# A list-scheduled linear-attention and MLP kernel: new per-unit delays, a new table of tile places and ten new scheduler constants

## The chip, the cores and the metric

One Trainium2 chip, of which the program uses 1 core. The metric is device time in microseconds (us) of that core. The profile shows one execution of the program; the times are of other executions of it.

## The reference

Linear attention with exponential features, then an MLP without bias. There are 8 batches, 8 heads, 576 positions, 64 channels per head and 128 random features; the MLP has 4608 tokens of 512 channels and 2048 hidden units.

```python
def phi(x):
    proj = np.einsum('bhsd,df->bhsf', x, w_phi)
    proj = proj - np.max(np.abs(proj), axis=-1, keepdims=True)
    return np.concatenate([np.exp(proj), np.exp(-proj)], axis=-1)
q_p, k_p = (phi(q), phi(k))
kv = np.einsum('bhsf,bhsd->bhfd', k_p, v)
z = np.sum(k_p, axis=2)
num = np.einsum('bhsf,bhfd->bhsd', q_p, kv)
den = np.einsum('bhsf,bhf->bhs', q_p, z)[..., None] + 1e-06
x = (num / den).transpose(0, 2, 1, 3).reshape(B * S, H * D)
h = x @ w_in
out = (0.5 * h * (1.0 + erf(h / sqrt(2)))) @ w_out
```

## The kernel before, in words

**Attention.** Heads go in pairs, so each batch b has four pairs, made of two groups g with two halves p each. For the keys of one (b, g, p), `k_quad` loads `kt` and `vt`, TensorE (PE) multiplies `kt` with the feature weights `wst` into the PSUM tile `pk`, VectorE (DVE) takes the largest absolute value `mx` and subtracts it (`ek`), ScalarE (ACT) makes both exponentials, and PE sums them with the values into the PSUM tile `kv`, which ACT copies to `kvn`. The last 64 positions of all heads of a batch go through `k_rest` first (`kr`, `pk_r`, `er`), and every `kv` begins with their part. For the queries, `q_front` loads `qt`, PE makes `pq`, ACT copies it to `pc`, GpSimd (POOL) finds the largest absolute value over the partitions (`mb`, a partition_all_reduce, line 539), DVE subtracts it from `pc` and ACT makes both exponentials `ef` (line 544). PE then makes the products `pn` with `kvn`, copied by ACT to `xo`; for the first three batches PE also makes the denominators `dn`, copied to `do`. For later batches GpSimd sums them (`db`, line 550). In a name such as pq_0_3_1 the numbers are batch, pair and half of the positions (keys: batch, group, half); `rest` is the last 64 positions. In batch 0 both halves have 288 positions, in the other batches the first half has 512.

**Weights.** They come as 64-bit numbers. `split_weight` takes one piece: a load `raw` (line 413), ACT's absolute value (line 416), four VectorE instructions (lines 417, 419, 421, 423) that make a 32-bit number `wt`, a rounded cast on ACT (line 395) and the remainder on VectorE (line 401). There are 16 pieces of `w_i` and 16 of `w_o`.

**MLP.** It works on 18 blocks of 256 tokens. In blocks 0 to 7 PE multiplies the tokens' high and low parts `xh`, `xl` with `w_i` into `ph`, ACT and VectorE make the gelu's high and low parts `gh`, `gl`, and PE multiplies these with `w_o` into `po`. Blocks 8 to 17 form the second product from seven smaller ones (`pa`, `pb`, with sums of weights `tw`). The first `ph` stands between the attention of batches 1 and 2, since it needs the tokens of batch 0 alone; from there on the attention's PE work lies between matmuls of the blocks.

**What sets the order.** No order is written out by hand. Each operation is recorded by `Plan.op` with its engine, a hand-set cost, the tiles that it reads and writes, and a rank, to which the delay of its unit of work is added (`k01` is the keys of batch 0, half 1; `q220` the queries of batch 2, pair 2, half 0; `w_o3` a piece of weights; `b5_1` a part of a block). `Plan.order` is a list scheduler over all engines: among the operations that can start, it takes the one of lowest rank, and `Plan.emit` writes the instructions of each engine in that order. SP's queue carries nearly all DMAs, in planned order too. `Plan.pool` says in which buffer a tile lies: in the one of its own tag, unless the table `HOME` names another.

```python
def new(shape, dt, name):
    home = HOME.get(name, tag)
...
o.rank += DELAY.get(self.unit, 0.0)
...
pq = ps["pp"]([P, 2, 512], F32, f"pq_{nm}")
...
acc = ps["kv"]([P, 4, D + 1], F32, f"kv_{nm}_{p}")
```

A tile has to wait until the one before it in its buffer has been read for the last time. During the attention the PSUM places are `ph` (two), `po`, `pp`, `kv` and `pn` (one each); a `pk` or `pq` lies in `pp`, a `kv` or `dn` in `kv`, a `pn` in `pn`, unless `HOME` says otherwise. In SBUF, the places of weights that haven't come yet (`w_i0_0` to `w_o15`) serve as buffers for tiles of the attention. So the table `HOME` decides which waits on a buffer there are, and the order of two tiles on PE decides which comes first in one place.

All matmuls are recorded at line 360, the tensor-tensor operations of VectorE at line 401, copies and casts at 395 and 397. The change touches only the tables and constants from line 934 on; the scheduler reads them in `Plan.op`, `Plan.pool` and `Plan.order`.

Of the kernel before, what the change touches and what calls it, by code (L numbers as in the profile page):

```python
# [315 lines left out]
def fused_kernel(ctx: ExitStack, tc: tile.TileContext, qT, kT, va, w_st, w_in, w_out, out):  # L316
# [693 lines left out]
}  # L1010
SEVEN = 8
SUMS = 2
SUMSAT = 175.933
SUMSEACH = 3.384
SUMSPAN = 581.86
T15 = 870.02
T18 = 997.68
BIAS = 551.516
STICK = 2
PATIENCE = 2.138  # L1020
URGE = -1000.0
EARLY = 41.32
WPACE = 4.989
# [5 lines left out]
LUMP = 82.289  # L1029
# [56 lines left out]
```

## Time and profile before

| what | value |
|---|---|
| times of three runs | 1045.68, 1046.75, 1046.44 us; median 1046.44 us |
| profiled execution | 1048.43 us; span 1046.6 us; 1.83 us around the span |
| mean granted TensorE clock in it | 0.993 of full |
| busy in the span | PE 1019.6, VectorE 661.1, ACT 614.5, GpSimd 276.9 us |
| moved from and to HBM | 75.87 MB read, 29.66 MB written |

The profiled execution took 1.99 us longer than the median. Busy times of different engines lie beside one another, so they don't add up to the span. "PE" is the time with a matmul in the array, "PEld" its loads of weights, which overlap matmuls. The granted clock is given as a share of 2.4 GHz: 1.00 is that, 0.50 is 1.2 GHz.

### The profile page before, as it was taken

How to read it: one execution, taken by the hardware profiler on the slowest of the kernel's cores; microseconds unless marked ns; L12 is line 12 of the kernel's file. 1: busy time of each engine (PE TensorE's matmuls, PEld its weight loads, DVE VectorE, ACT ScalarE, POOL GpSimd, SP SyncE). 2: the span in 40 equal slices, each digit the busy share in tenths (PEclk: the TensorE clock that was granted, in tenths of full speed). 3: DMA queues.
4: the chain of work that ended last, by engine and by line, in shares of the span. 5: the costliest groups of instructions: out<-in, count | busy, mean ns of one | idle time of the engine just before them, and what ended most of it. 6: DMA issues, size and time to landing. Idle time of an engine off the chain costs nothing.

```text
span 1046.6 us, 24197 instructions
## 1 busy us (share of the span) xinstructions
PE 1019.6 (97%) x10070; PEld 893.1 (85%) x10070; DVE 661.1 (63%) x1209; ACT 614.5 (59%) x1011; POOL 276.9 (26%) x72
## 2 busy tenths in 40 slices
PE   6889998999999999999999999999999999999998
PEld 5555776878878878897887889999999999999998
DVE  5899999987777854334643433555564556474754
ACT  5788888886768766757755642343243334243433
POOL 2343331373376352326566540000000000000000
PEclk9899999999999999999999999999999999999999
DMA  8775654524534433222321339201111111110000
GB/s 294 216 231 170 208 189 119 164 88 140 162 123 147 152 108 91 67 76 72 97 72 39 97 107 326 60 22 41 44 39 40 43 42 42 41 42 19 24 22 21
DMA packets 87327, 107.11 MB, mean 102 GB/s; under 512 B 29021, under 2 KB 57245, under 8 KB 87217
## 3 DMA queue, kind: packets, MB, share of 16 engines
q1 hardware_dynamic: 86928, 105.30, 32.7%
q8 instruction: 79, 1.29, 0.5%
q14 instruction: 32, 0.25, 0.1%
q10 hardware_dynamic: 288, 0.26, 0.1%
HBM read 75.87 MB, written 29.66 MB: 101 GB/s over the span
## 4 chain that ended last, share of the span: by engine, by line
PE 90%; DVE 5%; ACT 2%; issue 1%; DMA 1%; SPq 0%; DVEq 0%; ACTq 0%
PE ph L360 38%; PE po L360 17%; PE pa L360 10%; PE pb L360 7%; PE kv L360 6%; PE pn L360 4%; PE pk L360 3%; PE pq L360 3%; PE dn L360 1%; DVE wt_i L421 1%; PE pn_rest L360 1%; DMA vt<-in_va_dram 1%; DVE ek L401 0%; DVE wt_i L423 0%; DVE pc L401 0%
## 5 line engine op out<-in xcount | busy, mean ns | idle before, releaser
L360 PE MATMUL ph<-xh,w_i 128*128 128x256 f32 x2304 | 416.6, 278 | 0.0
L360 PEld LDWEIGHTS ph<-xh,w_i 128*128 128x128 f32 x2304 | 357.1, 188 | 9.0 <-issue 5.1
L360 PE MATMUL ph<-xl,w_i 128*128 128x256 f32 x1152 | 319.3, 277 | 0.0
L360 PEld LDWEIGHTS ph<-xl,w_i 128*128 128x128 f32 x1152 | 217.2, 189 | 0.3
L539 POOL PARTITION_ALL_REDUCE mb<-pc x36 | 120.6, 3356 | 202.3 <-ACT pc L395 153.3
L360 PE MATMUL po<-w_o,gh 128*128 128x512 f32 (+1 forms) x519 | 162.4, 395 | 0.0
L550 POOL PARTITION_ALL_REDUCE db<-pc x20 | 124.2, 6212 | 93.7 <-DVE pc L600 89.9
L360 PEld LDWEIGHTS po<-w_o,gh 128*128 128x128 f32 x519 | 93.3, 188 | 30.0 <-issue 8.5
L401 DVE TENSOR_TENSOR sg<-ga 128x256 f32<-128x256 f32 (+1 forms) x240 | 84.3, 376 | 54.1 <-ACT ga L839 50.3
L360 PE MATMUL pa<-w_o,oh 128*128 128x256 f32 x640 | 112.6, 276 | 0.0
L401 DVE TENSOR_TENSOR gl<-ph,gh 128x512 fp32r<-128x512 f32 x64 | 43.5, 687 | 90.7 <-ACT ph L750 90.6
L360 PE MATMUL po<-w_o,gl 128*128 128x512 f32 (+1 forms) x275 | 100.8, 378 | 0.0
L360 PEld LDWEIGHTS pa<-w_o,oh 128*128 128x128 f32 x640 | 96.3, 188 | 0.1
L839 ACT ACTIVATE ga<-ph 128x512 f32<-128x512 f32 x80 | 47.8, 597 | 82.3 <-PE ph L360 52.1
L401 DVE TENSOR_TENSOR ul<-sg,uh 128x384 fp32r<-128x384 f32 x80 | 44.6, 558 | 71.5 <-ACT uh L395 70.3
L360 PE MATMUL pa<-w_o,ol 128*128 128x256 f32 x320 | 88.3, 276 | 0.0
L360 PE MATMUL pb<-tw,uh 128*128 128x256 f32 x464 | 82.9, 276 | 0.1
L544 ACT ACTIVATE ef<-pc 128x1024 f32<-128x1024 f32 (+1 forms) x72 | 68.1, 973 | 14.2 <-DVE pc L401 10.3
L470 ACT ACTIVATE ek<-ek 128x1024 f32<-128x1024 f32 x64 | 67.6, 1059 | 11.1 <-DVE ek L401 10.2
L395 ACT CAST uh<-sg 128x384 fp32r<-128x384 f32 x80 | 41.0, 512 | 50.6 <-PE pb L360 25.3
L360 PEld LDWEIGHTS pb<-tw,uh 128*128 128x128 f32 x464 | 69.9, 188 | 0.3 <-DVE ob L401 0.3
L360 PE MATMUL pn<-ef,kvn 128*64 128x512 f32 (+1 forms) x288 | 64.9, 571 | 1.9 <-ACT do L395 0.8
(93 smaller groups left out, 1591.5 us busy)
## 6 DMA issues: line engine op xcount, KB each, us to landing
vt<-in_va_dram SPq DMA_DIRECT2D x32, 325.0 KB
t_d<-ts SPq DMA_DIRECT2D x40, 256.0 KB
out_dram<-ob SPq DMA_DIRECT2D x34, 256.0 KB
kt<-in_kT_dram SPq DMA_DIRECT2D x32, 256.0 KB
raw_i<-in_w_in_dram SPq DMA_DIRECT2D x16, 512.0 KB
raw_o<-in_w_out_dram SPq DMA_DIRECT2D x16, 512.0 KB
qt<-in_qT_dram SPq DMA_DIRECT2D x28, 256.0 KB
x_d<-xo SPq DMA_DIRECT2D x28, 256.0 KB
```

What stands on the lines that cost most here:

```text
L360: return tc.keep_in_program_order(nc.tensor.matmul(*a, **kw))
L395: op(eng, cost, lambda: nc.scalar.copy(out=dst(), in_=src()), r=r, w=w, **kw)
L401: op(eng, cost, lambda: e.tensor_tensor(out=dst(), in0=a(), in1=b(), op=o), r=r, w=w, **kw)
L421: op("dve", dve(512), lambda: v.scalar_tensor_tensor(out=t(), in0=low(), scalar=29, in1=t(), op0=ALU.logical_shift_right, op1=ALU.bitwise_ ...
L470: op("act", act(256 * n), lambda s=s: nc.scalar.activation(e[s](), e[1](), AF.Exp, scale=1.0 - 2.0 * s), r=[e[1]], w=[e[s]], table="exp", ...
L539: op("pool", plan.SPENT[most], lambda: nc.gpsimd.partition_all_reduce(mb(), pc(), P, bass_isa.ReduceOp.absmax), r=[pc], w=[mb], port=most, ...
L544: op("act", act(2 * n), lambda s=s: nc.scalar.activation(ef[s](), pc(), AF.Exp, scale=1.0 - 2.0 * s), r=[pc], w=[ef[s]], table="exp", **k())
L550: op("pool", plan.SPENT[total], lambda: nc.gpsimd.partition_all_reduce(db(), pc()[:, :2], P, bass_isa.ReduceOp.add), r=[pc], w=[db], port= ...
L839: op("act", act(2 * TB, True) + 0.037, lambda ph=ph, ga=ga: nc.scalar.activation(ga(), ph(), AF.Gelu), r=[ph_all], w=[ga], table="gelu", a ...
```

## The change

No operation is added, removed or reshaped. All 360 entries of `DELAY` have new numbers; of `HOME`'s 210 entries 33 stand as they were, and the new table has 224. Ten constants of the scheduler change. The diff is cut to the constants and to the lines of the tables that matter below; `q001` is the unit of the queries of batch 0, pair 0, second half.

```diff
 DELAY = {
...
-    "q030": -1607.8, "r00": -1909.3, "q001": -2026.1, "q011": -1929.5, "q021": -1199.6, "q031": -113.1, "r01": -1069.1, "w_i0_0": -1260,
+    "q030": -2405.8, "r00": -2479.3, "q001": -3437.1, "q011": -2634.2, "q021": -2588.7, "q031": -1127.7, "r01": -2527.4, "w_i0_0": -711.3,
...
 HOME = {
...
-    "kv_0_0_1": "ph", "kt_0_1_0": "gh", "vt_0_1_0": "ef", "kt_0_1_1": "w_o9", "vt_0_1_1": "pc", "mx_0_1_0": "w_o14", "ek_0_1_0_1": "w_o13",
...
-    "ef_1_0_0_0": "w_i1_2", "ef_1_0_0_1": "w_i0_2", "dn_1_0_0": "ph", "xo_1_0_0": "mb", "do_1_0_0": "mb", "qt_1_1_0": "w_i3_3", "pq_1_1_0": "po",
...
-    "kt_1_1_0": "xl", "vt_1_1_0": "db", "kt_1_1_1": "w_i3_2", "pk_1_1_0": "po", "mx_1_1_0": "w_o14", "ek_1_1_0_1": "w_i2_3", "ek_1_1_0_0": "w_i1_3",
...
-    "pc_2_2_0": "ek", "mb_2_2_0": "w_o12", "ef_2_2_0_0": "w_o14", "dn_2_2_0": "pn", "xo_2_2_0": "gh", "do_2_2_0": "pc", "pc_2_3_0": "mb",
...
+    "ek_0_0_1_1": "w_i1_3", "ek_0_0_1_0": "w_o8", "kv_0_0_1": "ph", "kt_0_1_0": "kt", "vt_0_1_0": "w_i2_3", "kt_0_1_1": "xl", "vt_0_1_1": "ef",
...
+    "do_0_3_0": "w_o15", "qt_0_0_1": "pc", "pq_0_0_1": "po", "pc_0_0_1": "ef", "mb_0_0_1": "w_o8", "ef_0_0_1_0": "w_i0_2", "ef_0_0_1_1": "w_i2_3",
...
+    "mb_0_3_1": "w_i1_2", "ef_0_3_1_0": "pc", "ef_0_3_1_1": "w_i0_3", "pn_0_3_1": "kv", "dn_0_3_1": "pn", "xo_0_3_1": "w_i2_2", "do_0_3_1": "w_i0_2",
...
+    "qt_1_0_0": "w_o11", "pq_1_0_0": "po", "pc_1_0_0": "w_o12", "mb_1_0_0": "w_o13", "ef_1_0_0_1": "xl", "pn_1_0_0": "kv", "xo_1_0_0": "w_o10",
...
-SUMSAT = 175.933
-SUMSEACH = 3.384
+SUMSAT = 174.271
+SUMSEACH = 2.354
...
-BIAS = 551.516
+BIAS = 702.831
...
-PATIENCE = 2.138
+PATIENCE = 2.126
...
-WPACE = 4.989
+WPACE = 5.047
...
-LUMP = 82.289
-LINGER = 6.494
+LUMP = 67.602
+LINGER = 6.464
...
-HOLD = 23.07
+HOLD = 21.532
...
-DMASLACK = 0.517
+DMASLACK = 0.686
```

Places of the tiles that the prediction names, where the table before or after says something else than the tag: pq_0_0_1 lay in `pp` and lies in `po`; dn_0_3_1 in `kv`, now `pn`; dn_2_2_0 in `pn`, now `kv`; dn_1_0_0 in `ph`, now `kv`; pn_1_0_0 in `pn`, now `kv`; vt_1_1_0 in `db`, now in the places of its own tag.

The order of the instructions moves on every engine up to about 190 us of the span before, and is the same from there on.

**ACT's queue at the first copy of key sums** (`kvn_0_0_0` is that copy; the last number of a name, here and below, only tells tiles apart). Before:

```order
L544 ACTIVATE ef_0_0_0_0_261<-pc_0_0_0_179 128x576
L544 ACTIVATE ef_0_0_0_1_263<-pc_0_0_0_179 128x576
L416 ACTIVATE wt_i0_0_266<-raw_i0_0_143 128x512
L395 COPY kvn_0_0_0_270<-kv_0_0_0_215 128x260
L416 ACTIVATE wt_i1_0_277<-raw_i1_0_147 128x512
L470 ACTIVATE ek_0_0_1_0_290<-ek_0_0_1_1_268 128x1024
L470 ACTIVATE ek_0_0_1_1_268<-ek_0_0_1_1_268 128x1024
```

and now:

```order
L544 ACTIVATE ef_0_0_0_0_257<-pc_0_0_0_175 128x576
L544 ACTIVATE ef_0_0_0_1_265<-pc_0_0_0_175 128x576
L416 ACTIVATE wt_i0_0_267<-raw_i0_0_141 128x512
L544 ACTIVATE ef_0_1_0_1_272<-pc_0_1_0_184 128x576
L416 ACTIVATE wt_i1_0_274<-raw_i1_0_145 128x512
L470 ACTIVATE ek_0_1_0_0_277<-ek_0_1_0_1_270 128x1024
L395 COPY kvn_0_0_0_282<-kv_0_0_0_216 128x260
L470 ACTIVATE ek_0_1_0_1_270<-ek_0_1_0_1_270 128x1024
L470 ACTIVATE ek_0_0_1_0_296<-ek_0_0_1_1_280 128x1024
```

The copy stood behind one piece of weights (L416); now one exponential for the queries (L544), a second piece of weights and one exponential for the keys (L470) stand ahead of it as well.

**SP's queue around the load of vt_1_1_0** (the values for the keys of batch 1, group 1, half 0). Before, where it was the 59th issue:

```order
L592 DMA d_d0_1_775<-do_0_0_1_768 4x144
L664 DMA dc_0_0_778<-d_d0_0_512 128x18
L712 DMA xr_0_521<-x_d0_3_0_666 128x256
L413 DMA raw_i2_1_828<-in_w_in_dram 128x512
L496 DMA vt_1_1_0_845<-in_va_dram 128x650
L477 DMA kr_2_849<-in_kT_dram 128x2x128
L563 DMA qt_1_1_0_867<-in_qT_dram 128x512
```

and now, where it is the 26th:

```order
L563 DMA qt_0_2_0_263<-in_qT_dram 128x288
L413 DMA raw_o0_291<-in_w_out_dram 128x512
L496 DMA vt_0_1_0_293<-in_va_dram 128x650
L494 DMA kt_1_0_0_309<-in_kT_dram 128x512
L496 DMA vt_1_0_0_311<-in_va_dram 128x650
L496 DMA vt_1_1_0_314<-in_va_dram 128x650
L477 DMA kr_1_316<-in_kT_dram 128x2x128
```

The load moved 33 places forward, out of a stretch of stores and weights into one of loads. Likewise `wst` was the 6th issue of the queue and is the 4th.

**PE's queue around the end of batch 2** (pk_3_0_0 and the like are the first keys of batch 3). Before:

```order
L360 MATMUL po_0_1403<-w_o11_2080,gl_0_5_2041 128x512
L360 MATMUL pk_3_0_0_2120<-wst_124,kt_3_0_0_1755 128x128 x8
L360 MATMUL pn_2_2_0_2134<-ef_2_2_0_0_2057,kvn_2_1_0_1870 64x512 x2
L360 MATMUL pn_2_2_0_2134<-ef_2_2_0_1_2082,kvn_2_1_0_1870 64x512 x2
L360 MATMUL dn_2_2_0_2155<-ef_2_2_0_0_2057,kvn_2_1_0_1870 32x256 x4
L360 MATMUL dn_2_2_0_2155<-ef_2_2_0_1_2082,kvn_2_1_0_1870 32x256 x4
L360 MATMUL pk_3_0_1_2175<-wst_124,kt_3_0_1_2140 128x128 x8
L360 MATMUL pn_2_3_0_2188<-ef_2_3_0_0_2173,kvn_2_1_1_2131 64x512 x2
L360 MATMUL pn_2_3_0_2188<-ef_2_3_0_1_2116,kvn_2_1_1_2131 64x512 x2
```

and now:

```order
L360 MATMUL pq_2_rest_2086<-qt_2_rest_1901,wst_120 128x256 x2
L360 MATMUL pn_2_2_0_2092<-ef_2_2_0_0_2036,kvn_2_1_0_1870 64x512 x2
L360 MATMUL pn_2_2_0_2092<-ef_2_2_0_1_2061,kvn_2_1_0_1870 64x512 x2
L360 MATMUL dn_2_2_0_2104<-ef_2_2_0_0_2036,kvn_2_1_0_1870 32x256 x4
L360 MATMUL dn_2_2_0_2104<-ef_2_2_0_1_2061,kvn_2_1_0_1870 32x256 x4
L360 MATMUL pk_3_0_0_2122<-wst_120,kt_3_0_0_1759 128x128 x8
L360 MATMUL po_0_1400<-w_o10_1948,gh_0_5_1987 128x512 x2
L360 MATMUL po_0_1400<-w_o10_1948,gl_0_5_2100 128x512
L360 MATMUL po_0_1400<-w_o10_1948,gh_0_5_1987 128x512 x2
```

The key projection pk_3_0_0 stood ahead of pn_2_2_0 and dn_2_2_0, with pk_3_0_1 directly behind them; now it stands behind them, and twelve `po` matmuls follow it before the next attention piece. Further on, pn_2_rest and dn_2_rest were followed by dn_2_3_0 and then kv_3_0_0; now dn_2_3_0 stands ahead of them and kv_3_0_0 directly behind.

## Rows read from the trace of the kernel before

**Rows 1.** The page's busy times, share of the span and instructions of each engine.

```profile
PE 1019.6 (97%) x10070; PEld 893.1 (85%) x10070; DVE 661.1 (63%) x1209; ACT 614.5 (59%) x1011; POOL 276.9 (26%) x72
```

**Rows 2.** Windows: stretch, length, busy of PE, PEld, DVE, ACT, POOL, clock, DMA, GB/s.

```profile
20.00:40.00 20.00, 15.84 (x354) 12.18 (x352) 19.68 (x28) 17.44 (x32) 4.67 (x2) 1.00 0.63 196
40.00:60.00 20.00, 18.34 (x296) 13.00 (x296) 15.85 (x25) 16.09 (x28) 7.18 (x3) 0.83 0.78 240
60.00:80.00 20.00, 16.93 (x272) 9.93 (x272) 18.98 (x24) 15.91 (x27) 9.73 (x3) 1.00 0.72 242
80.00:100.00 20.00, 17.76 (x201) 12.46 (x197) 18.64 (x27) 17.02 (x25) 9.62 (x3) 0.91 0.50 139
100.00:120.00 20.00, 20.00 (x231) 15.58 (x229) 18.99 (x33) 16.62 (x28) 4.31 (x1) 1.00 0.74 234
```

**Rows 3.** View of waits, engine PE, whole span: the costliest of 14 lines.

```profile
PE pk_r L360 <- DMA wst<-in_w_st_dram: 6.3, 1, 6.3
```

**Rows 4.** Timeline of PE: start, us, operation, count, idle before and releaser.

```profile
18.99 1.19 PE L360 MATMUL pn<-ef,kvn 128*64 128x288 f32 x8 [0.48 <-ACT kvn L395]
...
40.52 2.29 PE L360 MATMUL pq<-qt,wst 64*128 64x288 f32 x8 [2.95 <-DVE ek L401]
...
42.73 2.19 PE L360 MATMUL pn<-ef,kvn 128*64 128x288 f32 x8
...
47.47 0.69 PE L360 MATMUL kv<-vt,er 128*64 128x65 f32 x16
...
61.19 0.69 PE L360 MATMUL kv<-vt,er 128*64 128x65 f32 x16 [2.33 <-DMA vt<-in_va_dram]
...
70.05 0.70 PE L360 MATMUL dn<-ef,kvn 128*32 128x144 f32 x16 [1.32 <-ACT xo L395]
...
83.69 1.29 PE L360 MATMUL dn<-ef,kvn 128*32 128x256 f32 x16 [2.24 <-ACT do L395]
...
159.22 1.07 PE L360 MATMUL dn<-ef,kvn 128*32 128x256 f32 x16 [1.73 <-ACT xo L395]
...
160.95 1.16 PE L360 MATMUL pk<-wst,kt 64*128 64x128 f32 x16 [0.66 <-DVE ek L401]
...
166.97 0.69 PE L360 MATMUL kv<-vt,er 128*64 128x65 f32 x16 [0.61 <-ACT do_rest L395]
```

**Rows 5.** A window of 2 us (columns as in rows 2), of a half-clock stretch.

```profile
42.00:44.00 2.00, 2.00 (x10) 0.77 (x8) 1.06 (x2) 1.62 (x3) 1.39 (x1) 0.50 0.64 127
```

**Rows 6.** Timeline of ACT around the first copy of key sums.

```profile
17.34 0.69 ACT L416 ACTIVATE wt_i<-raw_i 128x512 f32<-128x512 f32 x1
...
18.56 0.38 ACT L395 COPY kvn<-kv 128x260 f32<-128x260 f32 x1 [0.53 <-PE kv L360]
...
39.27 1.26 ACT L544 ACTIVATE ef<-pc 128x576 f32<-128x576 f32 x2 [0.88 <-DVE pc L401]
...
40.43 1.04 ACT L470 ACTIVATE ek<-ek 128x1024 f32<-128x1024 f32 x1
```

**Rows 7.** Timeline of VectorE: an idle gap, and two long instructions beside plain ones.

```profile
46.98 0.43 DVE L417 TENSOR_SCALAR wt_o<-wt_o 128x512 f32<-128x512 f32 x1 [3.89 <-ACT wt_o L416]
...
66.36 2.67 DVE L421 SCALAR_TENSOR_TENSOR wt_o<-raw_o,wt_o 128x512 uint32<-128x512 uint32 x1
...
68.95 0.68 DVE L421 SCALAR_TENSOR_TENSOR wt_i<-raw_i,wt_i 128x512 uint32<-128x512 uint32 x1
...
70.16 3.20 DVE L401 TENSOR_TENSOR pc<-pc,mb 128x1024 f32<-128x1024 f32 x1
...
76.94 1.22 DVE L401 TENSOR_TENSOR pc<-pc,mb 128x1024 f32<-128x1024 f32 x1
```

**Rows 8.** Timeline of GpSimd: two reductions.

```profile
66.31 7.33 POOL L539 PARTITION_ALL_REDUCE mb<-pc  x2 [3.40 <-ACT pc L395]
```

**Rows 9.** Timeline of SP's queue: issues of two loads.

```profile
3.09 0.43 SPq L390 DMA_DIRECT2D wst<-in_w_st_dram  x1
...
55.61 0.85 SPq L496 DMA_DIRECT2D vt<-in_va_dram  x1
```

134 rows, old and new, of tables (DELAY, HOME) are left out of this document.

## The prediction

> **What bounds the kernel now.** I read the busy times first: TensorE (PE) has a matmul in the array for 1019.6 of 1046.6 us [rows 1]. So at most 27 us of the span are idle on PE, and the question is where they lie. The windows of 20 us answer it: between 100 and 120 us PE is busy for 20.00 of 20 us, but 15.84, 18.34, 16.93 and 17.76 in the four before it [rows 2]. What lies behind 190 us has the same order after the change, so I price nothing there. In the windows before 100 us VectorE is as full as PE or fuller: 19.68, 18.98 and 18.64 us, and only 15.85 between 40 and 60 [rows 2]. The reader should see from this that up to the first `ph` two engines bound the kernel in turn: a wait that goes on PE is worth nothing unless VectorE then also has its work earlier.
>
> The view of waits says that PE's costliest wait is its first, 6.3 us for `wst` [rows 3]. The timeline of PE gives the others in their places [rows 4]: 2.95 us before pq_0_0_1, at 40.52; 2.33 us for vt_1_1_0 before kv_1_1_0, at 61.19; 1.32 us before dn_0_3_1, at 70.05; 2.24 us before dn_1_1_0, at 83.69, just ahead of the first `ph`; in batch 2, 1.73 us before dn_2_2_0, 0.66 before pk_3_0_1 and 0.61 before kv_3_0_0. The clock comes third. From 42 to 44 us it is granted at 0.50, the lower level [rows 5], and the 20 us from 40 and from 80 have 0.83 and 0.91 of it, where the others shown have 1.00 [rows 2]; in both of these PE had one long wait, 2.95 and 2.24 us. Eight `pn` matmuls take 2.19 us there, against 1.19 at full clock [rows 4].
>
> **The change, part by part.** The prices are made against the profiled execution, 1048.43 us, 1.99 above the median of 1046.44.
>
> *Start.* `wst` was issued sixth, at 3.09 us [rows 9], and is now fourth; `kr`, which the same matmuls read, goes from third to fifth. An issue takes 0.43 us and a little more, so the later of the two is one place, about half a us, earlier. Bounds 0 and 0.9 us gained; I take 0.5 and count it in the next term.
>
> *First copy of key sums, kvn_0_0_0.* PE's pn_0_0_0 waits for it at 18.99 us [rows 4]. Before, ACT had waited 0.53 us for PE ahead of this copy, behind one piece of weights [rows 6]. Now three pieces stand in between: an `ef` of 0.63 us (half of 1.26), a piece of weights of 0.69 and an `ek` of 1.04 [rows 6]. 0.63 + 0.69 + 1.04 - 0.53 = 1.8 us later, and everything behind pn_0_0_0 on PE waits with it. Walking on through the four queues in the new order, with the durations of the rows, I get more such short waits, and kv_0_1_1, which closes the keys of batch 0, 2.9 us later. That is an estimate; the bounds are 1.3 (the 1.8 less the half us of the start) and 4 (twice the 1.8, and a little).
>
> *pq_0_0_1.* It lay in `pp` behind pk_1_0_0, which VectorE had to read twice; it now lies in `po`, which is long free. The 2.95 us go. If PE does not idle there, the low clock behind it goes too: the 20 us from 40 were granted 0.83, so 0.17 x 20 = 3.4 us of PE work [rows 2]. 2.95 + 3.4 - 2.9 = 3.4 us ahead at kv_1_0_0 (47.47 before [rows 4]), the largest lead that the change gives. VectorE allows it: it stood idle for 3.89 us up to 46.98 [rows 7], the one long gap it has there, and that gap hung on the late PE.
>
> *vt_1_1_0, dn_0_3_1.* The load moved 33 places ahead, past weights and stores; it had been issued at 55.61 us, 5.6 before its use [rows 4, 9], and is now there long before. The 2.33 us go. The load that moves back for it, vt_0_1_0 (14th to 23rd issue), is needed only by kv_0_1_0, and is in the 2.9 above. dn_0_3_1 lay in `kv` behind pn_0_3_1 and now has `pn`: 1.32 go. But VectorE is full again from 47 us, and its pieces set when PE has work. By the walk, kv_1_0_1 is 1.8 us ahead, kv_1_1_0 and kv_1_1_1 0.7 each: most of the 3.65 us comes back as waits for ACT and VectorE. pn_1_0_0 now stands in `kv` directly behind kv_1_1_1, and dn_1_0_0 behind pn_1_0_0, so each waits for ACT's copy of the one before it: new, estimated at 1 us each, under the 1.73 and 1.32 that such waits cost here [rows 4]. dn_1_1_0 still stands behind two copies. The first `ph` comes at 83.6 instead of 84.9 (where dn_1_1_0 started at 83.69 and took 1.29): a lead of 1.3. Bounds: -1.5 (half of the 2.9 late isn't made up) and +3.9 (VectorE's whole gap).
>
> *The low clock at 84 us.* The 20 us from 80 have 0.91, so 1.8 us are lost [rows 2]. Whether the clock falls depends on how long PE waits ahead of `ph`, and that wait is shorter but not gone. I take half, 0.9; bounds 0 and 1.8.
>
> *Batch 2.* dn_2_2_0 lies in `kv` now, away from pn_2_2_0: 1.73 go. pk_3_0_1 has twelve `po` matmuls between itself and pk_3_0_0: 0.66 go. Against that, kv_3_0_0 lies in `kv` directly behind dn_2_rest; before, dn_2_3_0 lay between them on PE, and still 0.61 was left [rows 4]. Without that cover, which took about as long as dn_2_2_0's 1.07 us, its wait grows to 0.61 + 1.07. Net 1.73 + 0.66 - 1.07 = 1.3 us. PE is full there, so these count one to one. Bounds 0.3 and 2.4 (no new wait).
>
> *Unseen short waits* between 90 and 190 us, where every engine's order moved: -0.5; bounds -2 and 0. The other new places in SBUF I price at nothing: what covers them is the work of VectorE, full nearly throughout; where a load came late behind such a place, the price would be of the kind of vt_1_1_0's 2.33.
>
> Sum: 1.3 + 0.9 + 1.3 - 0.5 = 3.0 us gained. Profiled 1045.4; median 1046.44 - 3.0 = **1043.4 us**.
>
> **A rule against it.** In the rows the clock fell in the two stretches with waits of 2.95 and 2.24 us, and stayed at 1.00 from 60 to 80 us, with waits of 2.33 and 1.32 us in it [rows 2, 4]. The change trades few long waits for more short ones, and by these rows that is good. The Trainium skill, page "TensorE: Matmul & The Clock Gate", section "A second HAM failure mode: psum-queue depth-cycling", says the contrary of such patterns: frequent micro-idles between groups of matmuls make the clock go up and down. By it, the two terms on the clock would be lost and the time would be that of the slower rival below. No row here shows a fall after short waits alone.
>
> **The rivals.** *Same time.* VectorE, at 18.6 to 19.7 of 20 us outside its one gap [rows 2], sets the pace to the first `ph` and beyond, its work is unchanged, and the lead of 3.4 is eaten: 0 at `ph`, 1.3 from batch 2, 0.5 to 2 back for the unseen waits: about 1046, and 1044.4 to 1048.4 with 2 us either way. For it speaks that every later piece of `ph` work needs VectorE; against it the gap of 3.89.
>
> *Slower.* The late kvn_0_0_0 costs its 2.9 us, the walk's recovery at pq_0_0_1 does not happen since PE, waiting for short pieces, keeps or regains the low clock once more (1.8 us, what it lost at 84): 2.9 + 1.8, less the 1.3 of batch 2, is 3.4 more, **1049.8**. It is decided at kv_1_0_0: if that starts later than 47.5 us, this holds. For it: the new order puts at least six tiles directly behind one another in a bank. Against: one such wait is an ACT copy, 0.38 us [rows 6], and what stands ahead of it.
>
> *A larger gain.* While GpSimd reduces, some VectorE instructions take far longer: an L421 2.67 us where the next one takes 0.68, an L401 3.20 where a later one of its shape takes 1.22, both beside the two reductions from 66.31 to 73.64 [rows 7, 8]. If the new order puts other instructions beside these reductions, 2.0 + 2.0 = 4.0 us of VectorE time come back before the first `ph`, VectorE no longer eats the lead there, and 3.0 + 4.0 gives **1039.4**. The Trainium skill, page "GPSIMD Engine Reference", section "Specifications", says that GpSimd shares its SBUF interfaces with VectorE, and that instructions in a two-port mode or with two SBUF inputs contend with it; the two named are of the second kind. Against it: no trace shows yet what stands beside a reduction after the change, and as many such instructions remain to be done in the same time.
>
> That the change does nothing is excluded: four queues have another order.
>
> **How the numbers follow.** My forecast 0.46 (its own range 1040.5 to 1045.5), same time 0.25, slower 0.19, larger gain 0.10. The range of 8 in 10 takes in the larger gain, with 2 us below it, and the price of the slower case: 1037.5 to 1050.0. A measurement here can tell 0.2%, 2.1 us. Faster by more: 0.40 of the forecast's 0.46 and 0.10 make 0.50. Within it: 0.06 and 0.22 of the same-time case make 0.28. Slower: 0.19 and 0.03 make 0.22.
>
> **What would show it.** Right: no wait before pq_0_0_1 and full clock from 40 to 47 us; kv_1_0_0 near 44; no wait for `vt`; first `ph` near 83.6; dn_2_2_0 without a wait, kv_3_0_0 with some 1.7. Wrong: low clock anywhere between 20 and 80 us, kv_1_0_0 behind 47.5, a first `ph` behind 84.9 (slower) or before 80 (larger gain), or a new wait behind 190 us, where I price nothing.

## The result, and the profile after

| kernel | executions | median | lowest to highest | ratio to before, 95% interval |
|---|---|---|---|---|
| before | 22 | 1046.60 us | 1042.79 to 1050.90 | |
| the change | 22 | 1055.32 us | 1046.46 to 1058.81 | 1.0070 [1.0051, 1.0090] |

The change makes the kernel 0.7% slower, well beyond the 0.2% that a measurement can tell. The forecast was 1043.4, its range ended at 1050.0. The profiled execution after took 1058.81 us (span 1057.0, mean clock 0.990).

More telling than the median is the spread. Over three jobs (the 22 above, and the runs r1_again and r2_again below) the changed kernel was executed 42 times: **12 took 1046.46 to 1050.98 us (the lower group), 30 took 1053.77 to 1058.98 (the upper group), and none lay between.** The medians of the two groups are 1048.73 and 1056.16. The 131 executions of the kernel before in the jobs of this study fill 1042.35 to 1052.56 us with no gap over 1.4 us. So the question has two parts: what splits the executions, and why even the lower group gains nothing.

PE's view of waits of the profiled execution (it belongs to the upper group), the costliest of 16 lines:

```profile
PE pn L360 <- ACT kvn L395: 7.7, 2, 4.8
PE pk_r L360 <- DMA kr<-in_kT_dram: 5.7, 1, 5.7
PE pq L360 <- DVE ek L401: 3.1, 1, 3.1
PE pq_rest L360 <- issue: 2.4, 1, 2.4
...
PE kv L360 <- ACT do_rest L395: 0.5, 1, 0.5
```

The first wait, 6.3 us before [rows 3], is now 5.7 and ends with `kr`. The waits for `vt` and of `dn` [rows 4] are gone, as forecast, and the 2.95 us before pq_0_0_1 are 0.60, now for its load. New are 7.7 us for `kvn` and 3.1 for an `ek`. Their places in PE's timeline:

```profile
19.52 1.79 PE L360 MATMUL pn<-ef,kvn 128*64 128x288 f32 x8 [2.94 <-ACT kvn L395]
...
57.49 1.33 PE L360 MATMUL pq<-qt,wst 64*128 64x288 f32 x4 [3.08 <-DVE ek L401]
...
79.35 3.68 PE L360 MATMUL pn<-ef,kvn 128*64 128x512 f32 x8 [4.77 <-ACT kvn L395]
```

They are pn_0_0_0, pq_0_3_1 and pn_1_0_0. Behind each of them PE is at the lower clock, behind the first from 20 to 23 us. Three windows of 2 us (columns as in rows 2):

```profile
42.00:44.00 2.00, 2.00 (x36) 1.47 (x30) 0.64 (x2) 2.00 (x6) 2.00 (x1) 1.00 0.96 343
...
60.00:62.00 2.00, 2.00 (x18) 0.82 (x18) 0.99 (x2) 1.77 (x4) 1.65 (x1) 0.50 0.87 226
...
80.00:82.00 2.00, 2.00 (x8) 0.48 (x4) 1.94 (x4) 1.43 (x3) 0.00 (x0) 0.50 0.84 288
```

The window from 42 us had 0.50 before [rows 5] and has 1.00 now: that part of the forecast came true. But low clock returned at 20, at 60 and at 80 us, and the forecast had named low clock anywhere between 20 and 80 us as a sign of being wrong.

The chain of waits from 46 to 92 us shows what made the two waits (some of its 51 pieces):

```profile
49.91 6.18 DMA x_d<-xo
...
56.21 1.24 DVE ek L401
...
57.53 1.06 ACT ek L470
...
62.52 3.34 PE kv L360 x80
...
70.34 1.55 DVE wt_i L419
...
73.68 3.14 DVE pc L401
...
76.89 0.92 issue
77.81 0.26 ACT ef L544
...
79.02 0.29 ACT kvn L395
...
79.35 3.68 PE pn L360 x8
```

Two things stand out. A store of 144 KB took 6.18 us to land, and a VectorE subtraction, an `ek`, waited 1.95 us for it, since it writes where the store still read. And an L419 and an L401 on VectorE took 1.55 and 3.14 us of the chain, where their plain durations are 0.42 and 1.22 us.

**The two groups side by side.** VectorE and GpSimd (its two L539 rows) in the profiled execution of the upper group:

```profile
67.86 1.23 DVE L465 TENSOR_REDUCE mx<-pk 128x8 f32<-128x1024 f32 x1 [0.54 <-PE pk L360]
69.11 1.22 DVE L401 TENSOR_TENSOR ek<-pk,mx 128x1024 f32<-128x1024 f32 x1
70.26 1.63 DVE L419 TENSOR_SCALAR wt_i<-wt_i 128x512 uint32<-128x512 uint32 x1
...
73.61 3.21 DVE L401 TENSOR_TENSOR pc<-pc,mb 128x1024 f32<-128x1024 f32 x1
76.73 0.68 DVE L401 TENSOR_TENSOR er<-pk_r,mx_r 128x512 f32<-128x512 f32 x1
...
68.07 3.54 POOL L539 PARTITION_ALL_REDUCE mb<-pc  x1 [5.04 <-ACT pc L395]
73.55 3.54 POOL L539 PARTITION_ALL_REDUCE mb<-pc  x1 [1.94 <-ACT pc L395]
```

and in the profiled execution of r1_again, the same kernel, of the lower group (span 1048.7 us; the last line is PE's pn_1_0_0):

```profile
66.46 1.22 DVE L465 TENSOR_REDUCE mx<-pk 128x8 f32<-128x1024 f32 x1
67.71 1.23 DVE L401 TENSOR_TENSOR ek<-pk,mx 128x1024 f32<-128x1024 f32 x1
68.85 0.48 DVE L419 TENSOR_SCALAR wt_i<-wt_i 128x512 uint32<-128x512 uint32 x1
69.26 0.68 DVE L423 SCALAR_TENSOR_TENSOR wt_i<-raw_i,wt_i 128x512 uint32<-128x512 uint32 x1
69.86 0.68 DVE L421 SCALAR_TENSOR_TENSOR wt_i<-raw_i,wt_i 128x512 uint32<-128x512 uint32 x1
...
71.06 1.21 DVE L401 TENSOR_TENSOR pc<-pc,mb 128x1024 f32<-128x1024 f32 x1
72.19 0.68 DVE L401 TENSOR_TENSOR er<-pk_r,mx_r 128x512 f32<-128x512 f32 x1
72.79 2.08 DVE L423 SCALAR_TENSOR_TENSOR wt_i<-raw_i,wt_i 128x512 uint32<-128x512 uint32 x1
...
66.87 3.72 POOL L539 PARTITION_ALL_REDUCE mb<-pc  x1 [3.92 <-ACT pc L395]
72.15 3.54 POOL L539 PARTITION_ALL_REDUCE mb<-pc  x1 [1.55 <-ACT pc L395]
...
74.97 1.94 PE L360 MATMUL pn<-ef,kvn 128*64 128x512 f32 x8 [1.80 <-ACT kvn L395]
```

This is where the two differ; that it makes the groups is tested by y1 below. In the execution of the lower group VectorE comes late to mx_1_1_1 (no wait), its L419 starts 1.98 us after the start of GpSimd's first reduction and takes 0.48; the subtraction of pc_1_0_0 starts 1.09 us ahead of the second reduction and takes 1.21. In that of the upper group VectorE is early, waits 0.54 us for PE, L419 starts 2.19 us after that start and takes 1.63. So the subtraction starts 0.06 us behind the second reduction and takes 3.21 us, 2.0 more than it needs alone; such an instruction is called held here. ACT's `ef`, its copy kvn_1_1_1 and PE's pn_1_0_0 hang on it; PE waits 4.77 us instead of 1.80 in r1_again and then runs at half clock: eight `pn` take 3.68 us instead of 1.94. The instruction held in the lower group's execution is an L423, a piece of weights behind the subtraction, on which nothing near depends.

What is held agrees with the Trainium skill, page "GPSIMD Engine Reference", section "Specifications" (GpSimd contends with VectorE instructions in a two-port mode or with two SBUF inputs): `pc` and L423 have two SBUF inputs, and `mx` and `ek`, which read PSUM, took their usual 1.2 us beside the first reduction. L419 has one input; no row shows in which mode it runs.

The traces show more: it matters which part of a reduction an instruction meets. Instructions with two SBUF inputs that started 0.06 to 1.07 us into a reduction of 3.54 us took so much longer that, with their plain time at the end, they were let go 2.05 or 2.06 us after its start (twelve profiles; for the `pc` above, 0.06 + 3.21 - 1.21). Those that started at 2.38 us or later, in a reduction of 3.54 or 3.72 us, took their plain time, as L423 and L421 at 69.26 and 69.86 us in the profile of r1_again. L419, started at 2.19 us, was let go at 3.40 (2.19 + 1.63 - 0.42).

### The profile page after: what moved, and what is told of

The parts are those of the page before. It is cut to its first block, busy times and chain, and to the rows that moved or that the text cites. A ratio compares the mean times of both kernels' runs of the same rounds, so it can differ in the third digit from the quotient of the medians.

```text
span 1057.0 us, 24220 instructions
## 1 busy us (share of the span) xinstructions
PE 1025.8 (97%) x10074; PEld 895.1 (85%) x10074; DVE 664.6 (63%) x1209; ACT 617.1 (58%) x1013; POOL 275.7 (26%) x72
## 4 chain that ended last, share of the span: by engine, by line
PE 89%; DVE 3%; DMA 3%; ACT 3%; issue 2%; SPq 1%; DVEq 0%; ACTq 0%
PE ph L360 37%; PE po L360 16%; PE pa L360 10%; PE pb L360 7%; PE kv L360 6%; PE pn L360 5%; PE pq L360 3%; PE pk L360 3%; DMA t_d<-ts 1%; PE dn L360 1%; ACT ek L470 1%; DMA x_d<-xo 1%; PE pk_r L360 0%; DVE ob L401 0%; DVE ek L401 0%
## 5 line engine op out<-in xcount | busy, mean ns | idle before, releaser
L539 POOL PARTITION_ALL_REDUCE mb<-pc x36 | 122.4, 3402 | 204.1 <-ACT pc L395 143.0
L401 DVE TENSOR_TENSOR sg<-ga 128x256 f32<-128x256 f32 (+1 forms) x240 | 84.6, 376 | 62.0 <-ACT ga L839 58.8
L401 DVE TENSOR_TENSOR gl<-ph,gh 128x512 fp32r<-128x512 f32 x64 | 43.5, 686 | 89.9 <-ACT ph L750 89.8
L401 DVE TENSOR_TENSOR ul<-sg,uh 128x384 fp32r<-128x384 f32 x80 | 44.6, 558 | 67.0 <-ACT uh L395 65.8
L470 ACT ACTIVATE ek<-ek 128x1024 f32<-128x1024 f32 x64 | 67.7, 1059 | 17.7 <-DVE ek L401 17.0
L360 PE MATMUL pn<-ef,kvn 128*64 128x512 f32 (+1 forms) x288 | 67.4, 589 | 9.2 <-ACT kvn L395 7.7
L544 ACT ACTIVATE ef<-pc 128x1024 f32<-128x1024 f32 (+1 forms) x72 | 67.9, 972 | 12.8 <-DVE pc L401 11.1
```

What stands on the lines that cost most here:

```text
L360: return tc.keep_in_program_order(nc.tensor.matmul(*a, **kw))
L401: op(eng, cost, lambda: e.tensor_tensor(out=dst(), in0=a(), in1=b(), op=o), r=r, w=w, **kw)
L470: op("act", act(256 * n), lambda s=s: nc.scalar.activation(e[s](), e[1](), AF.Exp, scale=1.0 - 2.0 * s), r=[e[1]], w=[e[s]], table="exp", ...
L539: op("pool", plan.SPENT[most], lambda: nc.gpsimd.partition_all_reduce(mb(), pc(), P, bass_isa.ReduceOp.absmax), r=[pc], w=[mb], port=most, ...
L544: op("act", act(2 * n), lambda s=s: nc.scalar.activation(ef[s](), pc(), AF.Exp, scale=1.0 - 2.0 * s), r=[pc], w=[ef[s]], table="exp", **k())
```

## The experiments

In all of them the order is the planned order of the named kernel, written out as a list, and only the shown line differs. Each job has its own executions of the kernel before, and the ratios are to those.

**r1_again, the change unchanged.**

> The changed kernel, unchanged, executed again for a second profile. Theory of the late store (T1): VectorE's subtraction for the keys ek_1_1_0_1 waits about 2 us for the store of xo_0_0_1 (it landed at 56.1 us in the first profile), PE waits about 3 us before pq_0_3_1, and the clock is low from about 57 to 64 us; median again about 1055 us. If this execution is one of the quick ones (1046 to 1050 us), the store lands before 54 us and the low clock at 57 to 64 us is missing. Theory of the clock alone (T4): the waits stand at the same places and are equally long in a quick and a slow execution, and only the stretches of low clock differ.

Measured: median 1056.13 us of 10 (1049.32 to 1058.98), before 1047.20 of 30: 1.0071 [1.0047, 1.0095]. Three executions in the lower group, seven in the upper; the profile, shown above, is of the lower. It has the wait of pq_0_3_1 (1.9 us, with low clock behind it from 58 to 61 us), the place of pn_1_0_0 and the wait of pq_rest (2.3 us) in common with the other one, but not the held subtraction. So the theory of the late store missed: it wanted the low clock at 57 us to be missing in a quick execution.

**x1_ek_place: `ek` away from the store.** In the change ek_1_1_0_1 lies behind xo_0_0_1, whose store it must wait for. Its own place is that of before; new is that xo_0_0_1 lies there too (before, in `pc`).

```diff
-    "ek_1_1_0_1": "w_i2_3"
+    "ek_1_1_0_1": "w_o7"
```

> One entry of the table of places: ek_1_1_0_1 no longer lies in w_i2_3 behind xo_0_0_1, but in w_o7, which nothing has used yet; the order of all engines is that of the changed kernel, written out. T1 (late store): no wait of PE before pq_0_3_1, no low clock from 57 to 64 us, kvn_1_1_0 at about 61 us in place of 65.9, first ph at about 86 in place of 89.9, time about 5 us less than the changed kernel: 1050 us. T2 (the PSUM place of pn_1_0_0): the 4.8 us before pn_1_0_0 stay, time within 2 us of the changed kernel. T3 (the PSUM place of pq_1_rest): the 2.4 us before pq_1_rest stay and set the time, within 2 us.

Measured: 1048.96 us (1046.98 to 1057.67), 1.0036 [1.0010, 1.0062]; three of 10 are still in the upper group, and one lies between the groups (1052.12). In its profile the wait before pq_0_3_1 is 0.7 us and PE has no low clock from 40 to 80 us. So the upper group is rarer without the store's wait, but not gone: the store is not what makes it.

**x2_pqrest_place: the `issue` wait of 2.4 us.**

```diff
-    pq_1_rest in the place of its tag, "pp"
+    "pq_1_rest": "po"
```

> One entry: pq_1_rest lies in po in place of pp, as in the kernel before; order as in the changed kernel, written out. T3: the 2.4 us before pq_1_rest and the low clock at 102 to 105 us (1.7 us) go, time 4 us less than the changed kernel: 1051 us. T1 and T2: 0 to 2 us less, since what is late ahead of it stays late, and the next piece of PE then waits for VectorE.

Measured: 1056.13 us (1046.24 to 1058.82), 1.0072 [1.0044, 1.0100]: nothing. In its profile the 2.4 us became a wait of 2.2 for `gl` at the same place. A miss.

**x3_pn_place: pn_1_0_0 away from kv_1_1_1.**

```diff
-    "pn_1_0_0": "kv"
+    pn_1_0_0 in the place of its tag, "pn"
```

> One entry: pn_1_0_0 lies in its own place pn in place of kv behind kv_1_1_1; order as in the changed kernel, written out. T2: the 4.8 us before pn_1_0_0 shrink to 1 or less, the low clock at 78 to 84 us goes (3.3 us), time 5 to 7 us less: 1049 us. T1: pn_1_0_0 then waits for its exponentials, which come at 77.9 us instead of the copy at 79.3, so 1.4 us less wait, 0 to 2 us of time.

Measured: 1051.08 us (1047.48 to 1054.95, 9 executions), 1.0037 [1.0012, 1.0062]; 4 of 9 above 1052. The place costs a little, since kvn_1_1_1 stands behind `ef` on ACT, but the long wait is for `ef` itself.

**x5_ek_pn_place: both.**

> Both ek_1_1_0_1 in w_o7 and pn_1_0_0 in pn, order of the changed kernel written out. If the store and the PSUM place are two links of one chain, each alone took away 7 and 5 us of the median and both together take away little more than the first: 1047 to 1049, and none over 1054. If they are two causes of their own, the sum: 1044 or less.

Measured: 1047.88 us (1046.87 to 1053.89), 1.0016 [0.9998, 1.0033]. The median is in the expected 1047 to 1049. One execution of 10 was in the upper group, and it was the profiled one: the subtraction started 0.06 us behind the second reduction there too, and took 3.21 us. PE's pn_1_0_0 now waited 3.4 us for `ef`.

**y1_pc_first: the subtraction two places earlier, nothing else.** VectorE's order:

```diff
+L401 TENSOR_TENSOR pc_1_0_0<-pc_1_0_0,mb_1_0_0
 L421 SCALAR_TENSOR_TENSOR wt_i1_1<-raw_i1_1,wt_i1_1
 L465 TENSOR_REDUCE mx_2_r<-pk_2_r
-L401 TENSOR_TENSOR pc_1_0_0<-pc_1_0_0,mb_1_0_0
```

> One instruction of VectorE moved in the changed kernel's order (all else written out as it was): the subtraction of pc_1_0_0 stands two places further forward, ahead of one weight instruction (L421) and of the maximum for pk_2_r. Theory of the meeting (R): in the slow executions this subtraction starts just after GpSimd's second reduction (73.61 behind 73.55) and takes 3.2 us in place of 1.2, and the copy of kvn_1_1_1 behind it makes PE wait 4.8 us; moved forward it no longer meets it, so the slow executions get 3 to 5 us shorter: median 1051 to 1053. Theory of the clock alone (T4): the low clock from 57 to 64 us sets the slow executions, and the subtraction takes 3.2 us because all is late; median stays at 1055 to 1056.

Measured: **1048.73 us** (1045.88 to 1050.58), before 1046.55: 1.0015 [1.0002, 1.0028]. None of 10 in the upper group; 0.7% of loss became 0.15%. Its profile (VectorE, then GpSimd):

```profile
66.32 1.23 DVE L465 TENSOR_REDUCE mx<-pk 128x8 f32<-128x1024 f32 x1 [0.52 <-PE pk L360]
...
68.72 1.63 DVE L419 TENSOR_SCALAR wt_i<-wt_i 128x512 uint32<-128x512 uint32 x1
70.27 0.67 DVE L423 SCALAR_TENSOR_TENSOR wt_i<-raw_i,wt_i 128x512 uint32<-128x512 uint32 x1
70.87 1.21 DVE L401 TENSOR_TENSOR pc<-pc,mb 128x1024 f32<-128x1024 f32 x1
...
66.53 3.54 POOL L539 PARTITION_ALL_REDUCE mb<-pc  x1 [4.26 <-ACT pc L395]
72.02 4.06 POOL L539 PARTITION_ALL_REDUCE mb<-pc  x1 [1.95 <-ACT pc L395]
```

VectorE waited for PE and its L419 was held, as in the upper group, but the subtraction was all but over when the second reduction began (it ended at 72.08 us, the reduction started at 72.02).

**y2_reduce_waits: the second reduction made to wait for the subtraction**, by the place of its result.

```diff
-    "mb_1_1_0": "w_o9"
+    "mb_1_1_0": "w_o13"
```

> One entry of the table of places in the changed kernel, order written out as it was: the result mb_1_1_0 of GpSimd's second reduction lies where mb_1_0_0 lay, so that this reduction cannot start before VectorE has made the subtraction of pc_1_0_0 that reads mb_1_0_0. No instruction of any queue moves. Theory of the meeting (R): pc_1_0_0 takes 1.2 us in every execution, none is slower than 1052, median 1048 to 1049 as with the moved instruction. Rival: moving the subtraction helped because it stood earlier by two instructions (1.4 us) in VectorE's queue, not because of the meeting; then here GpSimd's reduction is 1.2 us later and nothing is won: median 1055 or more.

Measured: 1051.76 us (1046.13 to 1055.24), 1.0049 [1.0030, 1.0069], between the two theories; five of 10 were above 1052, where the theory of the hold had expected none. In the profile the subtraction took 1.21 us, but pn_1_0_0 still waited 2.77 us, and its eight matmuls took 3.48, at half clock. L419 was still held and made the subtraction late; in y1 the two places made up for that. So to take the second hold away alone gives half of it.

**h1 and h2: front and rear apart.** h1 has the changed order up to what is planned for 260 us, and behind it the order of before; h2 the reverse.

> Order of the changed kernel for what its plan starts in the first 260 us, and from there on the order of the kernel before; table of places of the changed kernel. From the traces, all executions of the changed kernel lose another 2.4 to 2.9 us between 290 us and the end against the kernel before, quick and slow alike. If the order of the rear does that, this kernel is 2.6 us quicker than the changed one: median 1053, quick ones 1044 to 1047. If it is a consequence of the front (of when data come), it stays at 1055 to 1056.

> The reverse: order and places of the kernel before for the first 260 us, then the order of the changed kernel. If the order of the rear costs 2.6 us: median 1049.8 against 1047.2 for the kernel before in this job's runs, and none in the group above 1054. If the front alone makes the difference: within 1 us of the kernel before.

Measured: h1 1052.66 us (1043.78 to 1054.57), 1.0034 [1.0007, 1.0060], three executions at 1043.78 to 1046.19 and seven at 1052.19 or more; h2 1049.33 us (1045.57 to 1052.68), 1.0030 [1.0010, 1.0050]. So the rear alone costs 2.8 us (1049.33 less the 1046.55 of before in that job). The profiles say the same with less noise. From the start of ACT's copy kvn_4_1_1, near 290 us, to the end of the span it is 755.75 to 756.06 us in the five profiled kernels with the old rear (before, h1, b1, b2, c1), and 758.19 to 759.19 in the twelve with the new one: 2.7 us on average, with no difference between the groups. Behind kv_4_1_1 both orders have the same PE work left.

**b1_pc_first_old_rear and b2_all_four.** b1 is y1 with the old rear; b2 has the two places of x5 besides.

> The moved subtraction of pc_1_0_0 and, behind what the plan starts in 260 us, the order of the kernel before. If the two causes add up: 1048.7 less 2.7, median 1046.0, with no execution over 1050; within 1 us of the kernel before. If they share a cause: 1047.5 or more.

> The same with ek_1_1_0_1 in w_o7 and pn_1_0_0 in pn as well. If the store's wait is still worth what it costs PE in the first profile once the meeting is gone (a wait of 2 to 3 us and a low clock): 2 to 3 us less than with the moved subtraction and the old rear alone, median 1043.5 to 1044.5, quicker than both kernels. If VectorE sets the pace there anyway: within 1 us of it, 1045.5 to 1046.5.

Measured: b1 1047.84 us (1044.04 to 1050.75), 1.0015 [0.9999, 1.0032]; b2 1045.73 us (1043.34 to 1049.15), before 1046.13: 1.0000 [0.9986, 1.0014]. b1's rear is 2.2 us shorter than y1's in the profiles (756.06 against 758.23), but the ratios, uncertain by about 1.3 us each, are the same. By my expectation (1046.0 if the two add up, 1047.5 or more if not) they do not add up in the times; so the 2.7 us stand on the profiles and on h2, and b1's times do not confirm them. b2, expected at 1043.5 to 1044.5 if the store still cost something and at 1045.5 to 1046.5 if not, is level with before, and none of these kernels beats it.

**c1_before_reduce_waits: the same idea in the kernel before.** Its pc_1_0_0 is held too [rows 7, 8]. Here the second reduction waits for it.

```diff
-    "mb_1_0_0": "pc", "mb_1_1_0": "w_o10"
+    "mb_1_0_0": "w_o11", "mb_1_1_0": "w_o11"
```

> The kernel before, its order written out, with mb_1_0_0 and mb_1_1_0 both in w_o11, so that the second reduction waits for the subtraction of pc_1_0_0 here too (it took 3.20 us in the profile of before, at 70.16). If the meeting is paid in the kernel before as well: 1 to 2 us less, median 1045 to 1045.5, and its slower executions (1048 to 1050) get rarer. If it is hidden there, since PE has other work at hand (pn_1_0_0 lies in a place of its own): within 0.7 us of the kernel before.

Measured: 1047.27 us (1043.31 to 1049.28), 1.0002 [0.9985, 1.0019]: nothing, though the subtraction took 1.21 us in its profile instead of 3.20. In the kernel before, the hold is covered. Nor is it there in every execution: in h2's profile, which has the front of before, the subtraction took 1.21 us.

**The last job: is the held subtraction enough by itself?** y3 puts the subtraction two places later, behind er_2_1 and the L423 of wt_i1_1; kv0 puts ACT's copy kvn_0_0_0 ahead of ef_0_1_0_1 again, which undoes the forecast's first loss; r2 is the change once more.

```diff
 L465 TENSOR_REDUCE mx_2_r<-pk_2_r
-L401 TENSOR_TENSOR pc_1_0_0<-pc_1_0_0,mb_1_0_0
 L401 TENSOR_TENSOR er_2_1<-pk_2_r,mx_2_r
 L423 SCALAR_TENSOR_TENSOR wt_i1_1<-raw_i1_1,wt_i1_1
+L401 TENSOR_TENSOR pc_1_0_0<-pc_1_0_0,mb_1_0_0
```

> The change once more, unchanged, for a second look at it in the same job. If the meeting of pc_1_0_0's subtraction with GpSimd's second reduction decides, the times fall in the two groups of before, 1049 to 1051 and 1055 to 1059 us, and the profiled execution belongs to the upper group just when its subtraction takes over 3 us.

> The subtraction of pc_1_0_0 stands two places later on VectorE, behind er_2_1 and the L423 of wt_i1_1 (0.6 us each), so that it starts 1.2 us later, where the second reduction runs in nearly every execution. Theory of the meeting: nearly all executions are of the upper group, a median of 1055 to 1059 us, the subtraction takes over 2.5 us in the profile, and pn_1_0_0 waits over 3 us. Rival, that only the place in the queue counts: the median moves by the 1.2 us and the two groups stay, with some executions at 1050 to 1052.

> ACT copies kvn_0_0_0 ahead of ef_0_1_0_1, an exponential of half a pair, and so earlier. My step said that its delay of 1.8 us makes everything on PE late, 2.9 us by kv_0_1_1. If so, kv_0_1_1 closes 1 us or more earlier than in the change, and the meeting around 73 us comes at other times. Rival, from the trace after: kv_0_1_1 was only 1.1 us late, since VectorE and the loads set it; then pn_0_0_0's wait goes, kv_0_1_1 moves by under 0.5 us, and the median stays at 1055 to 1057.

Measured: r2 1055.06 us (1047.48 to 1056.70), three in the lower group and seven in the upper; y3 1055.66 us (1053.89 to 1057.12), all four in the upper group; kv0 1056.85 us (1054.98 to 1059.00), all four in the upper group. r2's profile is of the upper group, and the cleanest:

```profile
64.59 1.22 DVE L465 TENSOR_REDUCE mx<-pk 128x8 f32<-128x1024 f32 x1 [0.54 <-PE pk L360]
...
70.34 3.20 DVE L401 TENSOR_TENSOR pc<-pc,mb 128x1024 f32<-128x1024 f32 x1
...
70.28 3.54 POOL L539 PARTITION_ALL_REDUCE mb<-pc  x1 [1.94 <-ACT pc L395]
...
76.07 3.68 PE L360 MATMUL pn<-ef,kvn 128*64 128x512 f32 x8 [4.75 <-ACT kvn L395]
```

Here the store did no harm (pq_0_3_1 waited 0.67 us), and kvn_1_1_0 was copied at 62.64 us, 2.2 ahead of r1_again's 64.83. At kvn_4_1_1 it was 3.9 behind (293.94 against 290.04). So between these two executions 6.1 us were lost behind kvn_1_1_0, with no help from the store. In y3 my expectation missed in one point: the subtraction itself took 1.21 us, since the L423 ahead of it was held instead, 1.95 us. What counts is when the subtraction ends, not which instruction is held: it ended 9.3 us after the start of the first reduction (75.41 less 66.07), in r2 8.7, in y2 6.8, in y1 5.6 and in r1_again 5.4, and pn_1_0_0 waited 5.36, 4.75, 2.77, 1.80 and 1.80 us. No execution of y3 was in the lower group; with 12 of 42 of the change there, four executions are too few to show that it is gone.

The eleven profiled executions with the changed front and the changed rear, in one table (us); the last column is the time from the start of kvn_1_1_0's copy to that of kvn_4_1_1's, 226.5 before:

| execution | `mx` waits for PE | L419 | `pc` | pn_1_0_0 waits | its 8 matmuls | to kvn_4_1_1 |
|---|---|---|---|---|---|---|
| after | 0.54 | 1.63 | 3.21 | 4.77 | 3.68 | 232.5 |
| r2 | 0.54 | 1.63 | 3.20 | 4.75 | 3.68 | 231.3 |
| kv0 | 0.52 | 1.63 | 3.20 | 4.75 | 3.68 | 230.9 |
| x5 | 0.53 | 1.63 | 3.21 | 3.37 | 3.53 | 230.5 |
| y3 | 0.53 | 1.63 | 1.21 | 5.36 | 3.68 | 233.0 |
| y2 | 0.37 | 1.63 | 1.21 | 2.77 | 3.48 | 226.9 |
| y1 | 0.52 | 1.63 | 1.21 | 1.80 | 1.94 | 224.4 |
| r1 | none | 0.48 | 1.21 | 1.80 | 1.94 | 225.2 |
| x1 | none | 0.47 | 1.21 | 1.80 | 1.94 | 225.1 |
| x2 | none | 0.46 | 1.21 | 1.79 | 1.94 | 223.7 |
| x3 | none | 0.45 | 1.21 | 0.40 | 2.02 | 225.1 |

The late subtraction costs 5.3 to 9.3 us of the front (230.5 to 233.0 in the first five rows, 223.7 to 225.2 in the last five). And it comes when VectorE is *early*: in all seven profiles where `mx` has to wait for PE, L419 starts 2.19 us into the first reduction and is held; in the four where it has not, L419 starts at 1.98 to 2.00 us and is not. Which execution gets there hangs on some us of difference in the transfers and waits ahead of it (kvn_1_1_0's copy started at 62.15 to 65.91 us in these profiles); what makes that difference between executions was not settled.

## Why the prediction was wrong

The forecast misses by 11.9 us (1055.32 less 1043.4). From the groups and the rear: 6.6 are the upper group (1055.32 less 1048.73, the lower group's median), 2.7 the rear, and 2.6 are gains of the front that did not come even in the lower group.

**Right.** The start: PE's first wait fell from 6.3 to 5.7 us, 0.5 forecast. pq_0_0_1: of its 2.95 us 0.60 are left, the clock is 1.00 from 40 to 48 us, and kv_1_0_0 started at 43.73 us, 44 forecast. `vt`, dn_0_3_1 and dn_2_2_0 wait no more. kv_3_0_0 waits 0.54 us, where I had priced 1.68.

**kvn_0_0_0.** The size was right, and the reason was not shown. PE's kv_0_1_1 came 3.07 us later than before, 2.9 forecast (its main part, before and after):

```profile
26.89 2.04 PE L360 MATMUL kv<-vt,ek 128*64 128x65 f32 x64
```

```profile
29.96 2.04 PE L360 MATMUL kv<-vt,ek 128*64 128x65 f32 x64
```

But the copy was only 0.55 us late (19.11 less 18.56) and not 1.8, since kv_0_0_0 had ended 1.9 us earlier than before: there the clock was at 0.50 from 13 to 16 us, here it was not, which was not forecast. Counted from the end of kv_0_0_0, kv_0_1_1 started 8.4 us later before and 13.4 us later after. kv0 took PE's wait for the copy from 2.94 to 0.48 us, and there it was still 12.2 (32.08 less 19.93), with a median no lower. (The 1.1 us in kv0's expectation are the lateness of ACT's copy of kv_0_1_1, not of PE's work.) So at most some 1.2 of these 5 us hang on the copy, and what makes the rest stays open. That 2.9 came out was luck, and the lateness did no harm: kv_1_0_0 was ahead all the same.

**The step that failed** is the wait of pn_1_0_0 in "vt_1_1_0, dn_0_3_1", "estimated at 1 us". It was 4.77, and not because of the place: pn_1_0_0 also needs `ef`, and so the subtraction, which the second reduction held. The first `ph` started at 89.89 us (82.86 in r1_again, 83.6 forecast). With that went the term on the low clock at 84 us: behind pn_1_0_0's wait the clock was 0.50.

**Two smaller terms failed beside it.** "The other new places in SBUF I price at nothing: what covers them is the work of VectorE" did not hold for xo_0_0_1's place: VectorE itself waited 1.95 us for its store, and PE 3.08 behind that. I had read the load vt_1_1_0 and not asked which stores stand behind loads. And the "unseen short waits", -0.5, were too small: pq_1_rest alone waited 2.40 us (2.25 in r1_again), with low clock behind it. In x2 a wait of 2.2 us came in its place, so its cause stays open.

**The mechanism that I had as a gain.** The rival of a larger gain named the hold beside GpSimd's reductions, with its 2.0 us a time [rows 7, 8], and let the new order free VectorE of it. The price of one hold was right and the sign wrong. Before, ACT copied pc_1_1_0, which the second reduction reads, early, and PE hardly waited for pn_1_0_0; these are rows of ACT and of PE in the trace of before:

```profile
67.72 1.03 ACT L395 COPY pc<-pq 128x1024 f32<-128x1024 f32 x1
```

```profile
72.20 2.04 PE L360 MATMUL kv<-vt,ek 128*64 128x65 f32 x64
74.50 2.02 PE L360 MATMUL pn<-ef,kvn 128*64 128x512 f32 x8 [0.26 <-ACT ef L544]
```

So both reductions ran back to back, 66.31 to 73.64 us [rows 8]; the held subtraction ended at 73.36 [rows 7], and PE was busy with kv_1_1_1 until 74.24. The hold was covered, and c1 shows that to remove it gives nothing. The same copy after:

```profile
72.46 1.00 ACT L395 COPY pc<-pq 128x1024 f32<-128x1024 f32 x1
```

It now stands behind both `ek` exponentials of keys 1_1_1. So the second reduction starts 1.94 us after the end of the first, and the subtraction that it holds ends at 76.82 us, 2.2 after PE has ended kv_1_1_1 (74.58). I had looked at how long instructions are held, not at where the reduction begins and what covers its end. Both places were in the order to be read before the run.

**The slower rival** had the right side and the wrong mechanism, a late kvn_0_0_0 that is not made up: kv_1_0_0 passed its point of decision, 47.5 us, by 3.8 on the good side, and the loss came later.

**The rear.** "What lies behind 190 us has the same order after the change, so I price nothing there" is false, and so is the same sentence on the change ahead of the prediction: the order differs into the last blocks on PE, VectorE and ACT, up to some 840 us of the plan on SP's queue, and on GpSimd at four places near 500 us. (The constants that change are nine, not ten.) By the profiles it costs 2.7 us. In the trace of after PE has new waits there, for `ob` and `gl`, of 0.2 to 0.6 us each; they are less than half of the 2.7. Where the rest lies was not tested by an experiment of its own.

**The rule against it**, that frequent short waits make the clock go up and down, the traces neither refute nor make the cause. The rows of before held no fall after short waits alone, but r2_again has one: behind these two waits of under 1 us the clock was 0.50 from 58 to 60 us.

```profile
54.94 0.76 PE L360 MATMUL pq<-qt,wst 64*128 64x288 f32 x4 [0.67 <-DVE ek L401]
56.67 1.75 PE L360 MATMUL pn<-ef,kvn 128*64 128x288 f32 x8 [0.97 <-ACT ef L544]
```

x1's profile has the same two waits, 0.67 and 0.97 us, and kept 1.00; and x2's, with the changed front, had 1.00 throughout from 10 to 110 us. So many short waits need not lower the clock, and sometimes do. What separates the groups stands behind one longer wait: PE kept the higher clock behind pn_1_0_0's wait of 1.80 us, and lost it behind those of 2.77 us and more.

## What to carry to other kernels

When two engines share a resource, read where each of their pieces begins and what covers its end, and not only the sum of the stretched instructions: the same 2 us of hold cost nothing that can be measured in one order and, with the clock that fell behind it, over 5 us in the other. If the executions of one kernel fall in two groups, profile until there is one of each, and look for the first instruction whose duration differs; here moving one subtraction by two places removed the upper group. And compare the orders to the very end before calling a stretch the same.

## What was not expected of the hardware

- To be early was worse: where VectorE waited for PE (0.30 to 0.54 us, eight profiles), L419 started 2.19 us into a reduction and took 1.63 us, while at 1.98 to 2.00 us (six profiles) it took 0.45 to 0.48, and the reduction 3.72 us instead of 3.54.
- A hold does not last for the whole reduction: with two SBUF inputs an instruction was let go 2.05 us after the start of one of 3.54 us (3.20 us for a plain 1.21), and one that started at 2.38 us or later was not held.
- A store of 144 KB landed 6.18 us after its issue; loads of 512, 256 and 325 KB had been issued in the 3.7 us before it, and 247 GB/s moved on average from 40 to 60 us. That these loads made it late was not tested.
